# Second layers of experts 1 to 7 on column tiles of 64 and 32 tokens, in an attention and mixture-of-experts kernel

## The chip, the cores and the metric

The kernel runs on one core of a Trainium2 chip. The metric is the device time of one execution in microseconds (us); the time before is the median of three runs.

## The reference

Attention with normalised queries and keys feeds a mixture of experts that keeps, for each of 8 experts, the 80 tokens with the largest gate weight. All other rows of the output are zero.

```python
# q, k, v: (8, 12, 448, 64) f32;  x = attention output as (N=3584, D=768)
q_n, k_n = rmsnorm(q, g_q), rmsnorm(k, g_k)
attn = softmax(q_n @ k_n.T / sqrt(64));  x = attn @ v

logits = x @ w_gate                        # (3584, 8)
expert_idx = argmax(logits, axis=1);  gate_w = softmax(logits)[chosen expert]
for e in range(8):
    tok_idx = tokens of expert e, at most the 80 with the largest gate_w
    h = maximum(x[tok_idx] @ w1[e], 0)     # (80, 768) @ (768, 1024)
    out[tok_idx] = gate_w[tok_idx] * (h @ w2[e])   # (80, 1024) @ (1024, 768)
```

## The kernel before

The program has three stages. The first, about 350 us long, is the attention: it goes over 24 groups of four heads, with TensorE in tiles of 64 rows by 64 columns for the scores (`ps`) and the weighted values (`po`), and in tiles of 64 by 32 for the gate's logits (`zl`). Meanwhile GpSimd's queue brings the weights of experts 0 to 2 into SBUF as bf16 and stages those of experts 3 to 7 in DRAM as bf16 (`wb_scratch`, function `stage_w`). The second stage, some 12 us, ranks the tokens of the last batch, forms for each expert the list of its 80 tokens (`idxG`, `idxT`) and their gate weights (`gwT`), and picks expert 0's tokens with matmuls (`chosen`, tile `xT`). Matmuls called `busy` (tile `hot`) compute nothing that is used; they keep TensorE at work in the gaps.

The third stage is the loop over the experts, and the change lies there. For each expert e:

- `gather` fetches the 80 token rows (780 f32 each) from DRAM by an indirect DMA of GpSimd's queue, up to four experts ahead.
- `normal` scales the rows into bf16 (`xn`, three VectorE operations), and `xpose` turns them with six TensorE transposes (`pxt`) and a copy into `xgT`.
- First layer: 48 matmuls, w1's 128x128 blocks as weights and the 80 tokens as the moving side, into `ph`; ScalarE's Relu makes `h_sb` in two halves.
- Second layer: 16 matmuls, `h_sb`'s eight blocks (128 rows x 80 tokens) as weights and 384 columns of w2 as the moving side, into two `py` tiles of 80 x 384. Expert 7's runs as 32 matmuls of 192 columns.
- `weighted` multiplies by the gate weight on VectorE (`yo`), and `scatter` writes the 80 rows to the output by an indirect DMA.

All orders are those of the code; the schedule is manual, and each engine runs its instructions in that order. The weights of experts 6 and 7 go into the buffers of experts 0 and 1, in transfers of SyncE's queue that each wait until the old weights have been read (`fetch_late`). Their staged copies are written and read in the order (chunk, partition, column), so that one piece of DRAM is one row of a block: 2048 bytes for w1, 1536 for w2.

Of the kernel before, what the change touches and what calls it, by code (L numbers as in the profile page):

```python
# [21 lines left out]
def kernel(  # L22
# [41 lines left out]
    NW0 = 3  # L64
# [99 lines left out]
    def constants():  # L164
# [2 lines left out]
        nc.vector.tensor_scalar(numI[:, 1, :], rowI[:, :NJ + 1], 15, None, op0=ALU.bitwise_and)  # L167
        nc.vector.tensor_copy(numF[:, :, :], numI[:, :, :])

    onesb = tpool.tile([CAP, 128], BF16, name="onesb")  # L170
    nc.gpsimd.memset(onesb[:, :], 1.0)

# [26 lines left out]
    def load_weights(pool, e, slot, early=None):  # L199

        w1 = []
        for n, (c0, c1) in enumerate(((0, DC), ) if early is None else ((0, NE), (NE, DC))):
            if n == 0 and early is not None:
                w1.append(early)
                continue
            w1.append(pool.tile([128, c1 - c0, F], BF16, tag=f"w1_{slot}", name="w1_sb"))
        w2_sb = pool.tile([128, FC, DM], BF16, tag=f"w2_{slot}", name="w2_sb")
        w_tiles[e] = (w1, [w2_sb])

    def chunk(e, i, c):  # L210
        ts = w_tiles[e][i]
        return ts[0][:, c] if len(ts) == 1 or c < NE else ts[1][:, c - NE]
# [55 lines left out]
    with av_stack:  # L268
# [521 lines left out]
        def at_slot(where, s, f, *a):  # L790
            where.setdefault(s, []).append((f, a))
# [85 lines left out]
        for g in (NG - 2, NG - 1):  # L877
            at_slot(end, NS, xstore, g)
        at_slot(mid, 1, constants)
        for i in range(N // 128):  # L880
# [209 lines left out]
    for cs in (((3, 4, 1), (4, 5, 1)), ((0, 3, 0), )):  # L1090
# [7 lines left out]
        if cs[0][0]:  # L1098
# [8 lines left out]
    outs = dram_disjoint_views(out, E + 1)  # L1107
    xgs = {}
    def gather(e, wait=False):

        if e == 1:
            xgs[e] = tpool.tile([128, 1024], F32, tag="beat", name="xg")[:CAP, :XW]
        elif e % 4 == 3:
            xgs[e] = prep.tile([128, NJ + 1, 256], F32, tag="xb", name="xg")[
                :CAP].rearrange("p j d -> p (j d)")[:, :XW]
        else:
            xgs[e] = upool.tile([128, 2, S], F32, tag="us", name="xg")[:CAP].rearrange(
                "p u s -> p (u s)")[:, :XW]
        if wait:
            nc.vector.memset(xgs[e][:, 0:1], 0.0)  # L1120
        nc.gpsimd.indirect_dma_start(
            out=xgs[e], out_offset=None, in_=xr_dram[:, :],
            in_offset=bass.IndirectOffsetOnAxis(ap=idxG[:, e:e + 1], axis=0))

    gather(1)
    idxT = tpool.tile([CAP, E], U32, name="idxT")
    nc.vector.tensor_copy(idxT[:, :], psc[:CAP, 1, :E])
    idxL = tpool.tile([CAP, 2], U32, tag="move", name="idxL")
    for half in range(2):
        nc.vector.tensor_scalar(idxL[:, half:half + 1], psc[:CAP, 1, E - 1:E], 2.0, float(half),  # L1130
                                op0=ALU.mult, op1=ALU.add)
    gwT = tpool.tile([CAP, E], F32, name="gwT")
    nc.vector.reduce_sum(out=gwT[:, :], in_=psc[:CAP, 0, :3 * E].rearrange("p (c e) -> p e c", c=3),
                         axis=AX.X)
    busy(1)
    chosen(2, False)
    busy(1)
    for i in range(3):
        chosen(i, True)
    busy(2)  # L1140
    xgT = mpool.tile([128, DC, CAP], BF16, tag="xgT", name="xgT")

    def by_two(x, ps):
# [3 lines left out]

    by_two(xgT, [t[:, 0, :DC // 2 * CAP] for t in xT])
    xts = {0: xgT}
    ps_stack.close()  # L1150
    mps = ctx.enter_context(tc.tile_pool(name="moe_ps", bufs=2, space=PSUM, reuse_waits="tile"))


    def normal(e, behind=None):
        xg = xgs[e]
        xn = mpool.tile([CAP, DM], BF16, tag="xn", name="xn")
        for i in range(NQ):
            nc.vector.tensor_mul(*rows_normal(i, xn, xg))
            if behind and not i:
                behind()  # L1160
        return xn
# [15 lines left out]
            by_two(xgT, [first, pxt[:, :DC // 2].rearrange("p c t -> p (c t)")])  # L1177
        xts[e] = xgT

    def sums(pw):  # L1180
        return [mps.tile([CAP, pw], F32, tag=("py", "py", "pz", "pxt")[i], name="py",
                         bufs=2 if i < 2 else 1) for i in range(DM // pw)]

    pys = sums(DM // 2)
    for e in range(2, 4):
        gather(e, wait=(e == 2))
    for e in range(E):
        h_sb = mpool.tile([128, FC, CAP], BF16, tag="hsb", name="h_sb")
        for fh in range(2):
# [10 lines left out]
        if e + 1 < E and e != 1:  # L1200
            xn = normal(e + 1, (lambda: fetch_part(slice(FE, FC), True)) if not e else None)
        if 0 < e < E - 1:
            xpose(e + 1, xn)
        if e < E - 4:
            gather(e + 4, wait=True)
        DN = DM // 2
        yo = mpool.tile([CAP, DM], F32, tag="yo", name="yo", bufs=3)

        def scatter(half=None):
            if half is None:  # L1210
                o, at, y, n = outs[e], idxT[:, e:e + 1], yo[:, :], N
            else:
                o = outs[e + half].rearrange("n (h d) -> (n h) d", h=2)
                at, y, n = idxL[:, half:half + 1], yo[:, half * DN:half * DN + DN], 2 * N
            nc.gpsimd.indirect_dma_start(  # L1215
                out=o[:, :], out_offset=bass.IndirectOffsetOnAxis(ap=at, axis=0),
                in_=y, in_offset=None, bounds_check=n - 1, oob_is_err=False)

        pw = DN if e + 1 < E else DN // 2
        if e:  # L1220
            pys = sums(pw)

        def product(i, fcs):
            for fc in fcs:
                nc.tensor.matmul(pys[i][:, :], h_sb[:, fc, :],  # L1225
                                 chunk(e, 1, fc)[:, i * pw:i * pw + pw],
                                 start=(fc == 0), stop=(fc == FC - 1))

        def weighted(i):
            nc.vector.tensor_scalar(yo[:, i * pw:i * pw + pw], pys[i][:, :], gwT[:, e:e + 1],  # L1230
                                    None, op0=ALU.mult)

        if e + 1 < E:
            for fh in range(2):
                for i in range(2):
                    if not e and fh and i:
                        xpose(1, xn)
                    product(i, range(fh * (FC // 2), (fh + 1) * (FC // 2)))
            if not e:
                xn = normal(2)  # L1240
            for i in range(2):
                weighted(i)
            scatter()
        else:
            for fh in range(2):
                for i in range(2):
                    product(i, range(fh * (FC // 2), (fh + 1) * (FC // 2)))
                    if fh:
                        weighted(i)
            scatter(0)  # L1250
            for i in range(2, 4):
                product(i, range(FC))
                weighted(i)
            scatter(1)
        if NW0 + 3 + e < E:
            load_weights(wpool, NW0 + 3 + e, e)
            fetch_late(NW0 + 3 + e)


# [33 lines left out]
```

## Time and profile before

| | |
|---|---|
| median of three runs | 408.78 us (408.08 to 409.58) |
| the profiled execution's own time | 408.54 us |
| its span, first to last instruction | 406.8 us |
| busy, share of the span: TensorE matmuls | 97% |
| VectorE / ScalarE / GpSimd | 86% / 79% / 21% |
| granted TensorE clock, mean over the span | 0.996 |
| DMA over the span | 248 GB/s mean |

Busy shares are averages over stages with different limits. The loop over the experts takes the span's last 42 us, from 365 us on. The trace names each instruction by engine, line, operation and tiles; a matmul's recorded length holds its way through the array, so that starts are what tells the pace.

### The profile page before, as it was taken

The page shows a single profiled execution, that of the slowest core. Times are in us where ns is not written, and L with a number is a line of the kernel's source. Part 1 is how long each engine was busy: PE and PEld are TensorE (multiplying, and loading weights), DVE is VectorE, ACT ScalarE, POOL GpSimd, SP SyncE. Part 2 cuts the span into 40 slices and gives each one's busy share as a digit, 9 for nine tenths or more (in the row PEclk, how much of TensorE's full clock was granted, in tenths as well). Part 3 has the DMA queues.
Part 4 walks back from the last instruction along what each step waited for, and adds up shares of the span by engine and source line. Part 5 has one row for each costly group of instructions (what it writes and reads, how often), then busy time and mean ns, then how long its engine had stood idle before and what let it go on. Part 6 is the DMA issues. An engine that isn't in the chain of part 4 may idle for free.

```text
span 406.8 us, 12614 instructions
## 1 busy us (share of the span) xinstructions
PE 395.8 (97%) x5284; PEld 196.0 (48%) x5284; DVE 351.7 (86%) x655; ACT 321.2 (79%) x510; POOL 86.8 (21%) x142
## 2 busy tenths in 40 slices
PE   8999999999999999999999999999999999999994
PEld 7434444444444444444444443444444444468884
DVE  4899987998999999997999999979999977876552
ACT  5898979997989879987899789979897878482110
POOL 6200002401032012320251024010520020144422
PEclk9999999999999999999999999999999999999998
DMA  7358999999989999979999999999999459898991
GB/s 245 127 174 197 280 288 262 282 205 310 243 236 257 258 262 255 295 172 258 243 305 220 245 269 231 289 238 278 232 287 256 134 166 377 262 280 264 342 348 53
DMA packets 76041, 100.92 MB, mean 248 GB/s; under 512 B 8385, under 2 KB 65217, under 8 KB 75985
## 3 DMA queue, kind: packets, MB, share of 16 engines
q1 hardware_dynamic: 60176, 70.99, 54.2%
q0 software_dynamic: 15808, 29.13, 39.4%
q8 instruction: 41, 0.67, 0.6%
q14 instruction: 16, 0.12, 0.1%
HBM read 101.11 MB, written 39.89 MB: 347 GB/s over the span
## 4 chain that ended last, share of the span: by engine, by line
PE 73%; DVE 12%; ACT 8%; issue 5%; POOL 2%; POOLq 0%; DVEq 0%
PE ps L425 26%; PE po L442 25%; PE zl L477 5%; DVE sm L460 4%; PE tp L383 4%; PE xp L383 3%; DVE ms L316 2%; DVE qn L346 2%; PE py L1225 2%; PE wps L896 2%; POOL out_dram L1215 2%; ACT at L428 1%; PE ph L1194 1%; ACT qkT L414 1%; PE mp L668 1%
## 5 line engine op out<-in xcount | busy, mean ns | idle before, releaser
L428 ACT ACTIVATE at<-ps 128x896 f32<-128x896 f32 x168 | 146.5, 930 | 4.5 <-PE ps L425 3.3
L425 PE MATMUL ps<-qkT 64*64 64x448 f32 x1344 | 147.3, 548 | 2.5 <-ACT row L626 1.3
L442 PE MATMUL po<-at,vt 64*64 64x448 f32 x1344 | 142.5, 537 | 0.0
L460 DVE TENSOR_TENSOR sm<-sm,at 128x896 f32<-128x896 f32 x120 | 130.7, 1089 | 3.1
L442 PEld LDWEIGHTS po<-at,vt 64*64 64x64 f32 x1344 | 50.1, 133 | 74.0 <-issue 63.9
L425 PEld LDWEIGHTS ps<-qkT 64*64 64x64 f32 x1344 | 43.8, 132 | 66.6 <-issue 26.3
L316 DVE TENSOR_REDUCE ms<-sq 128x14 f32<-128x896 f32 (+1 forms) x50 | 52.0, 1042 | 6.8 <-ACT sq L309 6.7
L346 DVE TENSOR_TENSOR qn<-qk,rs 128x896 f32<-128x896 f32 (+1 forms) x47 | 50.6, 1078 | 1.3
L309 ACT ACTIVATE sq<-qk 128x896 f32<-128x896 f32 (+1 forms) x48 | 44.7, 930 | 2.1 <-DMA qk<-in_q_dram 1.1
L229 POOL COPY mark<-mark 1x1 bf16<-1x1 bf16 x18 | 7.1, 394 | 131.8 <-DVE mark L228 131.8
L745 ACT COPY xb<-xp 128x1024 f32<-128x1024 f32 x24 | 24.3, 1012 | 8.4 <-PE xp L383 8.1
L383 PEld LDWEIGHTS tp<-ident,qn 64*128 64x128 f32 x672 | 23.5, 139 | 12.1 <-issue 5.3
L383 PE MATMUL tp<-ident,qn 64*128 64x64 f32 x672 | 27.2, 226 | 0.3 <-DVE qn L346 0.3
L1198 ACT ACTIVATE h_sb<-ph 128x320 bf16<-128x320 f32 x16 | 7.0, 437 | 25.4 <-PE ph L1194 25.4
L449 ACT COPY us<-po 128x896 f32<-128x896 f32 (+1 forms) x24 | 21.4, 894 | 6.5 <-PE po L442 6.4
L458 DVE TENSOR_TENSOR sm<-at 128x896 f32<-128x896 f32 x24 | 26.0, 1083 | 0.1
L414 ACT COPY qkT<-tp 128x896 f32<-128x896 f32 x24 | 22.0, 917 | 3.6 <-PE tp L383 3.5
L412 ACT ACTIVATE qkT<-tp,gqk 128x896 f32<-128x896 f32 x23 | 23.6, 1025 | 0.0
L1225 PE MATMUL py<-w_sb,h_sb 128*80 128x384 bf16 (+1 forms) x144 | 22.4, 309 | 0.0
L1230 DVE TENSOR_SCALAR yo<-py,gwT 80x384 f32<-80x384 f32 (+1 forms) x18 | 10.0, 568 | 12.0 <-PE py L1225 11.9
L477 PE MATMUL zl<-us,wgs 64*32 64x448 f32 x192 | 20.3, 540 | 0.0
L477 PE MATMUL zl<-sm,zsel 64*32 64x448 f32 x192 | 20.1, 540 | 0.0
(202 smaller groups left out, 431.1 us busy)
## 6 DMA issues: line engine op xcount, KB each, us to landing
w_sb<-wb_scratch SPq DMA_DIRECT2D x8, 1536.0 KB, 11.5
vt<-in_v_dram SPq DMA_DIRECT2D x24, 448.0 KB, 7.1
out_dram<-zeros SPq DMA_DIRECT2D x28, 384.0 KB, 9.0
qk<-in_q_dram SPq DMA_DIRECT2D x23, 448.0 KB, 6.9
qk<-in_k_dram SPq DMA_DIRECT2D x23, 448.0 KB, 6.2
w_sb<-in_moe_w_dram POOLq DMA_DIRECT2D x6, 1536.0 KB, 15.2
xr_scratch<-xb SPq DMA_DIRECT2D x48, 192.0 KB, 6.8
wb_scratch<-in_moe_w_dram POOLq DMA_DIRECT2D x12, 768.0 KB, 9.7
```

The costliest lines, as they stand in the source:

```text
L309: nc.scalar.activation(o, x, AF.Square)
L316: nc.vector.reduce_sum(out=st[g]["ms"][:, a, lo:hi], in_=st[g]["sq%d" % a][:, lo:hi], axis=AX.X)
L346: e.tensor_mul(qn[:].rearrange("p (x hh) d -> p hh x d", hh=2)[:, h0:h1], qk[:, lo:hi].rearrange("p (hh x) d -> p hh x d", x=NX), rs[:, lo ...
L383: nc.tensor.transpose(o, w, one[p, p], tile_position=(p.start, 0))
L414: nc.scalar.copy(T[:], tp[:, :, :S])
L425: nc.tensor.matmul(ps[u * 64:u * 64 + 64, hh, :S], T1[d, u, x * 64:(x + 1) * 64], T0[d, u, :], start=True, stop=True)
L428: nc.scalar.activation(at[:], ps[:, :, :S], AF.Exp)
L442: nc.tensor.matmul(po[u][hh * D:(hh + 1) * D, u, :S], vt[p, hh * NX + x, :], at[p, hh, :], start=(x == 0), stop=(x == RD - 1))
L458: nc.vector.tensor_add(s["sm"][:], s["at0"][:], s["at1"][:])
L460: nc.vector.tensor_add(s["sm"][:], s["sm"][:], s["at%d" % x][:])
L477: nc.tensor.matmul(t[32 * c:32 * c + 32, r, :S], w, x, start=(i == 0), stop=(i == NQ - 1))
L1225: nc.tensor.matmul(pys[i][:, :], h_sb[:, fc, :], chunk(e, 1, fc)[:, i * pw:i * pw + pw], start=(fc == 0), stop=(fc == FC - 1))
```

## The change

**Second layers.** Experts 1 to 7 no longer use weights of 128 rows x 80 tokens. The first 64 tokens run as `main`: weights of 64 columns in two column tiles of the array, the left one for w2's columns 0 to 383, the right one for 384 to 767; both write one `py` tile of 128 partitions. The last 16 tokens run as `rest`, once for two experts (1 and 2, 3 and 4, 5 and 6): weights of 32 columns (tokens 48 to 79) in four column tiles, two for each expert, each with 384 columns of w2, into one `pz` tile. Expert 7's rest has four tiles of 192 columns. Tokens 48 to 63 are computed twice and are not written the second time: their row numbers are pushed out of bounds (`SKIP`).

**Lists.** Gate weights and row numbers are needed in the new partition order. Six f32 matmuls with slices of the identity spread them (`spread`), ahead of expert 0's first layer; one `busy` matmul there goes.

**Order.** The gathers of experts 2 and 3 come after the first half of expert 0's first layer (a VectorE copy that reads `ph`). `normal(e + 2)` stands in expert e, ahead of the product's scaling. Expert 7's w2 is fetched after expert 2's rest, in two parts.

**DRAM layout.** The staged weights of experts 6 and 7 lie as (partition, chunk, column): one run of 12288 bytes for each partition.

```diff
+    MT = 64
+    LT = CAP - 32
+    SKIP = float(1 << 17)
     def staged(e, i):
-        return wb_dram[e - NW0, i].rearrange("(c p f) -> p c f", p=128, c=(DC, FC)[i])
+        return wb_dram[e - NW0, i].rearrange(
+            "(p c f) -> p c f" if e >= E - 2 else "(c p f) -> p c f", p=128, c=(DC, FC)[i])
...
+    psp = [hot[-1][:, 1, :2 * E], hot[-1][:, 1, 2 * E:3 * E]]
+    for o, c in enumerate((slice(0, MT), slice(LT, CAP))):
+        n = c.stop - c.start
+        for p in range(0, 128, n):
+            es = slice(1 + p // 64, None, 2) if o else slice(0, E)
+            nc.tensor.matmul(psp[o][p:p + n].rearrange("p (c e) -> p c e", c=2), ident[:CAP, c],
+                             rows[:, :, es], start=(o == 0), stop=(o == 1))
...
+    def main(e, py, fcs):
+        for fc in fcs:
+            for n in range(2):
+                product(py[MT * n:MT * n + MT, :], e, fc, slice(0, MT),
+                        slice(n * DN, n * DN + DN))
+
+    def rest(parts, pz, fcs):
+        w = len(parts) * DM // 4
+        for fc in fcs:
+            for n in range(4):
+                e, c = parts[n * len(parts) // 4], n % (4 // len(parts)) * w
+                product(pz[32 * n:32 * n + 32, :w], e, fc, slice(LT, CAP), slice(c, c + w))
...
+            if e == fh == 0:
+                gather(2, ph[:CAP, 0, 0:1])
+                gather(3)
...
+        if 0 < e < E - 2:
+            xn = normal(e + 2)
...
         else:
+            py = sums("py")
+            main(e, py, fcs)
+            yo = mpool.tile([128, DN], F32, tag="yo", name="yo", bufs=3)
+            nc.vector.tensor_scalar(yo[:, :], py[:, :], gws[:, e:e + 1], None, op0=ALU.mult)
+            scatter(e, idxM[:, e:e + 1], yo[:, :], 2)
+        if e and (e % 2 == 0 or e == E - 1):
+            k = (e - 1) // 2
+            pair = (e - 1, e) if e < E - 1 else (e, )
+            w = len(pair) * DM // 4
+            pz = sums("pz")
+            rest(pair, pz, fcs)
...
+        elif e == 2:
+            w2 = wpool.tile([128, FC, DM], BF16, tag="w2_1", name="w2_sb")
+            w_tiles[E - 1][1].append(w2)
+            for c in (slice(0, FE), slice(FE, FC)):
+                nc.sync.dma_start(out=w2[:, c], in_=staged(E - 1, 1)[:, c])
```

On TensorE, at the end of expert 2's second layer, the program before has these rows (py_6102 and py_6103 are its two halves of 80 x 384; LDWEIGHTS loads the weights of the matmul below it; ph_6126 is expert 3's first layer):

```order
L1225 LDWEIGHTS h_sb_6032
L1225 MATMUL py_6102<-w2_sb_125,h_sb_6032 80x384
L1225 LDWEIGHTS h_sb_6032
L1225 MATMUL py_6103<-w2_sb_125,h_sb_6032 80x384
...
L1194 LDWEIGHTS w1_sb_5200
L1194 MATMUL ph_6126<-xgT_6089,w1_sb_5200 128x80
```

The changed program has there (py_6129 is expert 2's main tile, py_6151 the rest tile of experts 1 and 2; w2_sb_124 and h_sb_5967 are expert 1's, w2_sb_126 and h_sb_6060 expert 2's):

```order
L1225 LDWEIGHTS h_sb_6060
L1225 MATMUL py_6129<-w2_sb_126,h_sb_6060 64x384
L1225 LDWEIGHTS h_sb_5967
L1225 MATMUL py_6151<-w2_sb_124,h_sb_5967 32x384
L1225 LDWEIGHTS h_sb_5967
L1225 MATMUL py_6151<-w2_sb_124,h_sb_5967 32x384
L1225 LDWEIGHTS h_sb_6060
L1225 MATMUL py_6151<-w2_sb_126,h_sb_6060 32x384
```

Sixteen rows of 80x384 for each expert have become sixteen of 64x384 for each and thirty-two of 32x384 for the two, and the w2 of the expert before is still read here.

On VectorE, from the end of the second stage into expert 1, the program before has these rows (L1158 is `normal`, L1146 and L1175 are `xpose`'s copies, L1120 the write that a gather waits for, L1230 the scaling):

```order
L1133 TENSOR_REDUCE gwT<-psc 80x8
L1146 CAST xgT<-xT 128x240
L1120 MEMSET xg 80x1
L1158 TENSOR_TENSOR xn<-xg 80x2x2x64
L929 MEMSET w_sb 128x1
L1158 TENSOR_TENSOR xn<-xg 80x2x2x64 x2
L1120 MEMSET xg 80x1
L1146 COPY xgT<-pxt 128x240
L1158 TENSOR_TENSOR xn<-xg 80x2x2x64 x3
L1230 TENSOR_SCALAR yo<-py,gwT 80x384 x2
L1175 COPY xgT<-pxt 128x480
```

And the changed program, from the same place on (L1135 is the copy that holds back the gather of expert 2, L1189 `normal`, L1279 the scaling of expert 0, L1286 that of a main):

```order
L1168 CAST xgT<-xT 128x240
L1172 COPY spread<-hot 128x24
L1175 TENSOR_SCALAR idxM<-spread,off 128x8
L1179 TENSOR_SCALAR idxP<-spread,off 128x3
L1179 TENSOR_SCALAR idxP<-spread,off 128x1
L1135 COPY xg<-ph 80x1
...
L1279 TENSOR_SCALAR yo<-py,rows 80x384 x2
L1206 COPY xgT<-pxt 128x480
L1133 MEMSET xg 80x1
L1189 TENSOR_TENSOR xn<-xg 80x2x2x64 x3
L1286 TENSOR_SCALAR yo<-py,spread 128x384
```

The write that released expert 2's gather has become a copy that must wait for `ph`, and in expert 1 the rows of expert 3 are normalised ahead of expert 1's scaling.

On GpSimd's queue each scatter of a main or a rest has 128 row numbers, of which those of the tokens computed twice are out of bounds; there are 12 scatters (one of expert 0, seven of mains, four of rests) in place of 9.

## Rows read from the trace of the kernel before

**Rows 1.** Window of expert 3: each engine's busy time and instructions.

```profile
378.80:383.40 4.60, 4.60 (x77) 3.85 (x74) 2.68 (x9) 0.88 (x2) 2.13 (x2) 1.00 1.04 307
```

Columns: the window and its length, then PE, PEld (weight loads), DVE, ACT, POOL, each with its instructions, the granted clock (1.00 is full), the DMA engines' busy share, and GB/s.

**Rows 2.** The chain that ended last: start and length in us, what.

```profile
344.69 1.50 PE po L442 x16
...
369.67 1.72 PE ph L1194 x48
371.39 0.22 PE pxt L1173 x6
371.61 2.60 PE py L1225 x16
```

**Rows 3.** Timeline around 344 us, TensorE alone: start, length, engine, line, operation.

```profile
342.96 1.73 PE L425 MATMUL ps<-qkT 64*64 64x448 f32 x16
344.51 1.68 PE L442 MATMUL po<-at,vt 64*64 64x448 f32 x16
346.13 0.18 PE L668 MATMUL mp<-eqb,tied 128*128 128x8 bf16 x1
...
346.77 0.56 PE L477 MATMUL zl<-us,wgs 64*32 64x448 f32 x1
...
347.93 0.54 PE L477 MATMUL zl<-sm,zsel 64*32 64x448 f32 x1
...
348.43 1.74 PE L442 MATMUL po<-at,vt 64*64 64x448 f32 x16
```

The tile's form stands ahead of the operand's: 64*32 is 64 rows by 32 columns of the array.

**Rows 4.** Timeline, all engines: weight loads of the zl matmuls and of 80 columns.

```profile
346.80 0.11 PEld L477 LDWEIGHTS zl<-sm,zsel 64*32 64x32 f32 x2
...
353.61 0.40 PEld L710 LDWEIGHTS <-keep 80*80 80x80 bf16 x8
```

**Rows 5.** Timeline ahead of expert 0's first layer.

```profile
364.41 0.60 PE L603 MATMUL hot<-tri,identb 128*128 128x512 bf16 x2
...
364.61 0.41 DVE L1146 CAST xgT<-xT 128x240 bf16<-128x240 f32 x1 [0.28 <-PE xT L1082]
...
364.91 1.93 PE L1194 MATMUL ph<-xgT,w_sb 128*128 128x80 bf16 x48
```

**Rows 6.** Timeline of gathers 2 and 5, expert 2's `normal`, and expert 3's scaling.

```profile
365.31 0.90 POOL L1121 DMA_INDIRECT xg<-xr_scratch,idxG  x1 [1.11 <-DVE xg L1120]
...
369.25 1.08 DVE L1158 TENSOR_TENSOR xn<-xg 80x256 bf16<-80x256 f32 x3
...
372.93 0.93 POOL L1121 DMA_INDIRECT xg<-xr_scratch,idxG  x1 [0.30 <-issue]
...
382.72 1.26 DVE L1230 TENSOR_SCALAR yo<-py,gwT 80x384 f32<-80x384 f32 x2 [1.54 <-PE py L1225]
```

**Rows 7.** DMA issues, last number us to landing: gathers 2, 4, 5; expert 7's w2.

```profile
xg<-xr_scratch,idxG POOLq DMA_INDIRECT x1, 3.5
...
xg<-xr_scratch,idxG POOLq DMA_INDIRECT x1, 8.6
...
xg<-xr_scratch,idxG POOLq DMA_INDIRECT x1, 7.6
...
w_sb<-wb_scratch SPq DMA_DIRECT2D x1, 1536.0 KB, 22.9
```

**Rows 8.** Timeline of SyncE's last transfer and of the tail.

```profile
374.24 1.95 SPq L244 DMA_DIRECT2D w_sb<-wb_scratch  x1
...
398.62 2.87 PE L1225 MATMUL py<-w_sb,h_sb 128*80 128x192 bf16 x32
...
399.88 0.74 DVE L1230 TENSOR_SCALAR yo<-py,gwT 80x192 f32<-80x192 f32 x2 [2.16 <-PE py L1225]
...
400.90 0.92 POOL L1215 DMA_INDIRECT out_dram<-yo,idxL  x1 [1.99 <-DVE yo L1230]
401.53 0.41 DVE L1230 TENSOR_SCALAR yo<-py,gwT 80x192 f32<-80x192 f32 x1 [0.25 <-PE py L1225]
402.84 0.92 POOL L1215 DMA_INDIRECT out_dram<-yo,idxL  x1 [1.02 <-DVE yo L1230]
```

More of the change, by code (lines that the diff above doesn't have):

```diff
@@ L879 @@
         at_slot(mid, 1, constants)
+        at_slot(mid, 3, offsets)
         for i in range(N // 128):
@@ L1106, with gather @@
             chosen(1, False)
-    outs = dram_disjoint_views(out, E + 1)
+    outs = dram_disjoint_views(out, E + E // 2)
     xgs = {}
-    def gather(e, wait=False):
+    def gather(e, behind=None, wait=False):
         if e == 1:
@@ L1120, in gather @@
             nc.vector.memset(xgs[e][:, 0:1], 0.0)
+        if behind is not None:
+            nc.vector.tensor_copy(xgs[e][:, 0:1], behind)
         nc.gpsimd.indirect_dma_start(
@@ L1125 @@
     gather(1)
[L1126 to L1134, printed above, removed]
+    idxT = tpool.tile([CAP, 1], U32, name="idxT")
+    nc.vector.tensor_copy(idxT[:, :], psc[:CAP, 1, :1])
+    rows = tpool.tile([CAP, 2, E + 1], F32, tag="move", name="rows")
+    nc.vector.tensor_copy(rows[:, 1, :E], psc[:CAP, 1, :E])
+    nc.vector.reduce_sum(out=rows[:, 0, :E],
+                         in_=psc[:CAP, 0, :3 * E].rearrange("p (c e) -> p e c", c=3), axis=AX.X)
+    nc.vector.tensor_copy(rows[:, :, E:], rows[:, :, E - 1:E])
+    gwT = rows[:, 0]
     busy(1)
@@ L1178, in xpose, with sums, scatter, product @@
         xts[e] = xgT
[L1180 to L1186, printed above, removed]
+    DN = DM // 2
+    def sums(tag, p=128, n=DN):
+        return mps.tile([p, n], F32, tag=tag, name="py", bufs=2 if tag == "py" else 1)
+    def scatter(k, at, y, h):
+        o = outs[k] if h == 1 else outs[k].rearrange("n (h d) -> (n h) d", h=h)
+        nc.gpsimd.indirect_dma_start(
+            out=o[:, :], out_offset=bass.IndirectOffsetOnAxis(ap=at, axis=0),
+            in_=y, in_offset=None, bounds_check=h * N - 1, oob_is_err=False)
+    hs = {}
+    def product(o, e, fc, t, c):
+        nc.tensor.matmul(o, hs[e][:, fc, t], chunk(e, 1, fc)[:, c],
+                         start=(fc == 0), stop=(fc == FC - 1))
+    def main(e, py, fcs):
[6 more added lines that the diff above has]
+        for fc in fcs:
+            for n in range(4):
+                e, c = parts[n * len(parts) // 4], n % (4 // len(parts)) * w
+                product(pz[32 * n:32 * n + 32, :w], e, fc, slice(LT, CAP), slice(c, c + w))
+    pys = [sums("py", CAP) for _ in range(2)]
     for e in range(E):
         h_sb = mpool.tile([128, FC, CAP], BF16, tag="hsb", name="h_sb")
+        hs[e] = h_sb
         for fh in range(2):
@@ L1205 @@
             gather(e + 4, wait=True)
[L1206 to L1231, printed above, removed]
@@ L1233 @@
-        if e + 1 < E:
+        if 0 < e < E - 2:
+            xn = normal(e + 2)
+        fcs = range(FC)
+        if e == 0:
+            yo = mpool.tile([CAP, DM], F32, tag="xo", name="yo", bufs=1)
             for fh in range(2):
                 for i in range(2):
-                    if not e and fh and i:
+                    if fh and i:
                         xpose(1, xn)
-                    product(i, range(fh * (FC // 2), (fh + 1) * (FC // 2)))
-            if not e:
-                xn = normal(2)
+                    for fc in fcs[fh * (FC // 2):(fh + 1) * (FC // 2)]:
+                        product(pys[i][:, :], e, fc, slice(0, CAP), slice(i * DN, i * DN + DN))
+            xn = normal(2)
@@ L1241 @@
             for i in range(2):
-                weighted(i)
-            scatter()
-        else:
[L1245 to L1257, printed above, removed]
+                nc.vector.tensor_scalar(yo[:, i * DN:i * DN + DN], pys[i][:, :], gwT[:, :1],
+                                        None, op0=ALU.mult)
@@ new lines @@
+            scatter(0, idxT[:, :1], yo[:, :], 1)
+        else:
+            py = sums("py")
[9 more added lines that the diff above has]
+            rest(pair, pz, fcs)
+            last = e == E - 1
+            yr = mpool.tile([128, DN], F32, tag="yo" if last else "yr", name="yr",
+                            bufs=3 if last else 1)
+            nc.vector.tensor_scalar(yr[:, :w], pz[:, :w], gwP[:, k:k + 1], None, op0=ALU.mult)
+            scatter(E + k, idxP[:, k:k + 1], yr[:, :w], 4 // len(pair))
```

28 lines of the change are left out of this document (25 added, 3 removed).

## The prediction

> **What bounds the kernel now.** I read the windows first, because the change touches the loop over the experts and little else. In the window of expert 3 TensorE is busy 4.60 of 4.60 us at a granted clock of 1.00, while VectorE has 2.68, ScalarE 0.88 and GpSimd 2.13 us of work [rows 1]. So TensorE sets the pace of an expert. The chain that ended last says how its 4.5 us divide: 1.72 for the first layer, 0.22 for the transposes, 2.60 for the second layer [rows 2]. Sixteen matmuls in 2.60 us are 162.5 ns each, the time to stream 384 columns; every one of them costs that, with 80 columns of weights or with 32.
>
> The DMA engines come second: in the same window their share is 1.04 [rows 1], that is, full. Their last work that matters is expert 7's w2, issued at 374.24 and landed 22.9 us later, at 397.1, and its reader starts at 398.62 [rows 7, 8]. TensorE can thus gain 1.5 us ahead of expert 7 before this transfer could hold it, even if the new layout gives nothing. In the tail neither bounds: the last scatter starts at 402.84, 0.90 us after its data is ready (401.53 and 0.41), and the one ahead of it at 400.90 [rows 8].
>
> **The change part by part.**
>
> *Streams.* What the main and the rest cost depends on whether column tiles that share all rows of the array run at once. No bf16 matmul of 128 rows does this here, but the gate's logits come near: tiles of 64x32, four of them side by side on the same rows, eight at once. Three rounds of eight take 347.93 - 346.77 = 1.16 us, 0.387 each [rows 3]; the sixteen `po` of 64x64 tiles, four at once, add 1.50 to the chain [rows 2], 0.375 for a round of four. So four column tiles of a row group do run together, at some 3% more than a stream. Two or four tiles of bf16 should then take the 162.5 ns of one matmul, and up to 10 ns more: I take 170. The weight loads fit: eight loads of 80 columns lie within 0.40 us, a recorded length of about 0.1 us included, some 43 ns apart [rows 4], and four of 32 columns have 162 ns. A main is 8 rounds, 1.36 us; a rest is 8 rounds, 1.36 us, for two experts. Two experts now cost 5.20 us of second layers, and then 2 x 1.36 + 1.36 = 4.08: 1.12 less. Three pairs give **-3.36** (at 162.5 ns -3.90, at 180 ns -2.64).
>
> *Changes of form.* The program now goes from whole to 64-column to 32-column tiles and back. A pair has five such changes (two for the odd expert, three for the even one), three pairs have 15. The attention has such seams: from `po` to a whole-array matmul 346.13 - 344.51 - 1.50 = 0.12 us, from `zl` to `po` 348.43 - 347.93 - 0.375 = 0.125 [rows 3]. But `ps` to `po`, with no change of form, also takes 1.55 us for 1.50 of streams, 0.05 [rows 3]. So a change costs between 0.07 and 0.125; I take 0.11, near the two seams that do change. 15 x 0.11 = **+1.65** (1.05 to 1.9).
>
> *Ahead of expert 0.* Six small f32 matmuls in two forms replace one `busy`. The second `busy` streams until about 364.84 (two of 0.21 from 364.41), and the first layer starts at 364.91 and waits for VectorE's copy until 365.02 [rows 5]. Three changes of form at 0.11 and six matmuls at 0.04 (the spacing of the small loads in [rows 4]) are 0.57; without the 0.21 of the `busy`, TensorE comes 0.36 later, of which 0.07 to 0.18 were idle. **+0.2** (0 to 0.5). The lists' own VectorE operations come behind that copy, and ahead of `normal(1)`, which waits for its gather; they are hidden.
>
> *The later gather 2.* It was issued at 365.31, and took 3.5 us, landing at 368.8; `normal(2)` ran at 369.25 [rows 6, 7]. Now it waits for half a first layer of a later expert 0, and starts at about 366.7. With 3.5 us it lands at 370.2, 0.9 us past 369.25 (less about 0.2 by which all is later). `normal(2)` is then late; behind it on VectorE stand expert 0's two scalings, and the first main needs the PSUM buffer that the first of these frees. Before, that buffer was free about 0.6 us ahead of its use (369.25 + 1.08 + half of an operation pair of 1.26 is 370.96, against a second layer that starts at 369.67 + 1.72 + 0.22 = 371.6). So the stall is 0 to 0.3 at that length, nothing if the gather, alone on the queue now, lands sooner, and up to 0.85 if it takes 4.2 or so. **+0.1** (0 to 0.85).
>
> *Order of `normal`.* It stands an expert earlier on VectorE, ahead of a scaling. Gather 5, issued at 372.93 with 7.6 us [rows 6, 7], lands at 380.5; its new place comes at about 380, and its transposes at about 383.2. A late gather now holds back a scaling too, but the next main has a second PSUM buffer. Nothing.
>
> *Expert 7 and the tail.* From the start of its second layer to the last scatter it was 402.84 - 398.62 = 4.22 us. Now: a change 0.11, main 1.36, about 0.2 through the array, a scaling of 0.6 (half of the 1.26 of [rows 6]), 0.28 to the scatter, as from 400.62 (399.88 and 0.74) to 400.90 before [rows 8]: main's scatter at 2.55. The rest's last data is ready at about 3.2 (eight rounds of four loads, 0.10 to 0.13 each). Its scatter then waits for GpSimd: the two scatters before stood 1.94 apart, and two gathers can stand 1.2 apart. That is 3.75 to 4.49, against 4.22. A scatter of 128 row numbers in place of 80 may take 0.92 to 1.47 us. Together -0.5 to +0.8; **0**, between the ends.
>
> *DRAM layout, constants.* Longer runs may bring the weights sooner; nothing waits for them (above), so 0. If w2 came at the old time and TensorE gained more than 1.5 us, the cover would end, but its first part (six of eight blocks) lands earlier, and the last two are read 1 us into the main. The constants are 16 small GpSimd writes in the attention, where GpSimd is busy 21% of the span.
>
> Sum: -3.36 + 1.65 + 0.2 + 0.1 + 0 = **-1.4**. The profiled execution took 408.54, so 407.1; the median of the runs stands 0.24 higher, so **407.4**.
>
> **The rivals.**
>
> *The seams eat it.* With 180 ns a round, 0.125 a change, 0.5 ahead of expert 0, 0.5 at gather 2 and +0.5 in the tail: -2.64 + 1.9 + 1.5 = +0.8, 409.5; with half of these, about 408.4. For it: each is within its bounds. Against: all must lean one way.
>
> *Cheaper seams.* 0.07 a change, 162.5 ns, and 1.2 us between the last scatters: -3.9 + 1.05 + 0.1 - 0.5 = -3.2, 405.5. Against it: both seams with a change of form show 0.12.
>
> *Starved gathers (the other side).* A gather lands 3.5 us after its issue on quiet DMA engines, and 7.6 to 8.6 beside the weights [rows 7]. The weights' pieces of 1.5 to 2 KB become runs of 12 KB. If a gather's pieces must then wait longer between them, gathers 4 to 7 land late. Gather 5's transposes leave it about 9 us (383.2 - 1.1 - 372.9); each microsecond of landing beyond is one of stall for `xpose`, where TensorE waits with nothing behind it that it may do. At 10.4 us the gain is gone, at 11.6 the kernel is 0.3% slower, and at 13 it is 411.2. Against: the bytes are the same, and the queue of weights then ends sooner. The Trainium skill, "DMA: Bandwidth & Descriptors", section on queues, rings and completion order, has each DMA engine take turns between queues packet by packet, which speaks for this rival; the trace has no long packets beside gathers, so no run here shows it.
>
> *Tiles one after another.* If a weight load waited for the matmul on the same rows, each small matmul would cost its stream and its load: main 16 x 0.19, rest 32 x 0.19, 12.2 us for a pair in place of 5.2: +21 for three pairs, and expert 7's +4, near 434. Against: the loads of `zl`'s next round stand at 346.80, while the first round, on the same rows, runs until 347.17 and beyond [rows 3, 4]. By the Trainium skill, "TensorE: Matmul & The Clock Gate", Part 3, loads overlap matmuls in flight only when the row group differs, which would be this rival; the trace does not agree.
>
> **How the numbers follow.** Forecast 0.50 (406.4 to 408.2), seams 0.22, cheaper seams 0.13, starved 0.12, one after another 0.03. About 0.3%, 1.2 us, is what a measurement here can tell from no change. The forecast's 0.50 splits 0.37 to 0.13 at 407.55; cheaper seams are all faster; the seams are 0.18 same and 0.04 slower; starved 0.02 same and 0.10 slower. Faster 0.50, same 0.33, slower 0.17. For 8 in 10 the range leaves out the far ends of starved gathers and the last rival, 0.1, and a tail of the cheap end, 0.1: **405.6 to 409.9**.
>
> **What would show it.** Right: mains of about 1.36 us and rests of about 1.36, with starts of the two or four tiles together; seams of 0.1; TensorE without gaps from expert 1 on; expert 7's second layer about 1.4 us earlier. Wrong: a wait of transposes for `xn` and behind it for a gather; a start of expert 7's main that waits for w2; last scatters 2 us apart or more; starts of column tiles one stream apart.

## The result and the profile after

The changed kernel took 412.58 us (median of four runs, 412.18 to 412.83), the kernel before beside it 408.66 (408.08 to 409.58): a ratio of 1.0084, 95% interval 1.0057 to 1.0111. It is slower by 0.8%; the forecast had it 0.3% faster. The profiled execution took 412.54 us, 4.0 more than that of before, with a span of 410.8 and a granted clock of 0.998.

The timeline of the changed kernel, rows of the loop over the experts (start, length, engine, line; in brackets the idle time before it and what ended it). L1250 is the first layer, L1225 main and rest, L1204 the transposes, L1189 `normal`, L1206 the copy into `xgT`, L1297 the scaling of a rest, L1136 a gather, L1218 a scatter:

```profile
365.21 1.90 PE L1250 MATMUL ph<-xgT,w_sb 128*128 128x80 bf16 x48
366.70 0.91 POOL L1136 DMA_INDIRECT xg<-xr_scratch,idxG  x1 [2.44 <-DVE xg L1135]
...
372.11 1.49 PE L1225 MATMUL py<-w_sb,h_sb 128*64 128x384 bf16 x16 [0.20 <-DVE yo L1279]
...
373.54 1.90 PE L1250 MATMUL ph<-xgT,w_sb 128*128 128x80 bf16 x48
374.13 0.93 POOL L1136 DMA_INDIRECT xg<-xr_scratch,idxG  x1 [0.30 <-issue]
...
376.37 2.90 PE L1225 MATMUL py<-w_sb,h_sb 128*64 128x384 bf16 x48
...
377.79 1.09 PEld L1225 LDWEIGHTS <-h_sb 128*32 128x32 bf16 x32 [0.30 <-issue]
...
379.21 0.46 PE L1250 MATMUL ph<-xgT,w_sb 128*128 128x80 bf16 x8
...
383.76 0.93 POOL L1136 DMA_INDIRECT xg<-xr_scratch,idxG  x1 [0.30 <-issue]
...
385.73 1.09 DVE L1189 TENSOR_TENSOR xn<-xg 80x256 bf16<-80x256 f32 x3 [3.97 <-DMA xg<-xr_scratch,idxG]
...
386.21 0.92 PE L1204 MATMUL pxt<-identb,xn 80*128 80x80 bf16 x6 [1.65 <-DVE xn L1189]
...
394.64 0.62 DVE L1297 TENSOR_SCALAR yr<-py,spread 128x384 f32<-128x384 f32 x1 [2.00 <-DMA out_dram<-yr,idxP]
395.17 0.40 DVE L1206 COPY xgT<-pxt 128x480 bf16<-128x480 bf16 x1
395.62 1.88 PE L1250 MATMUL ph<-xgT,w_sb 128*128 128x80 bf16 x48 [1.78 <-DVE xgT L1206]
...
397.16 1.09 DVE L1189 TENSOR_TENSOR xn<-xg 80x256 bf16<-80x256 f32 x3 [1.59 <-DMA xg<-xr_scratch,idxG]
...
403.15 2.27 PE L1225 MATMUL py<-w_sb,h_sb 128*64 128x384 bf16 x48
...
405.58 0.98 POOL L1218 DMA_INDIRECT out_dram<-yo,idxM  x1 [2.26 <-DVE yo L1286]
406.86 0.98 POOL L1218 DMA_INDIRECT out_dram<-yr,idxP  x1 [0.30 <-issue]
```

TensorE's work came out as the sum had it. A main runs from 372.11 to 373.54, 1.43 us with the change of form behind it; a main and a rest from 376.37 to 379.21, 2.84. The time went to waits that were not there before. Expert 5's rows are normalised only at 385.73, when their gather of 374.13 has landed, and TensorE stands 1.65 us ahead of the transposes. At 394.64 a rest's scaling waits 2.00 us for the scatter that still reads its buffer; the copy into `xgT` is queued behind it on VectorE, and the first layer of expert 6 stands 1.78 us. Where `xn` comes late the six transposes also follow `normal`'s three operations two by two and take 0.8 to 0.9 us (386.21) in place of 0.4; this happens four times, for experts 3, 5, 6 and 7, and is some 2 us more. From the first layer of expert 0 to expert 7's second layer it is 37.94 us (365.21 to 403.15), against 33.71 before [rows 5, 8]; the tail, to the last scatter, is 3.71 against 4.22. The loop's stretch is thus 4.23 longer, and with the tail and a start 0.30 later, 4.23 - 0.51 + 0.30 = 4.0, which is the whole difference.

What the gathers cost, in the view of the tile `xg` of the changed kernel (idle time of VectorE, and all recorded landings):

```profile
  DMA xg<-xr_scratch,idxG: 15.5, 7
...
DMA to landing us min/median/max: 3.6/9.9/12.6
```

Before, VectorE waited 2.2 us, once, for a gather. The DMA issues of the changed kernel, last number us to landing: gathers 2, 5 and 6, the scatter of the first rest (issued 382.45), the last part of expert 7's w2 (issued near 379.8):

```profile
xg<-xr_scratch,idxG POOLq DMA_INDIRECT x1, 3.6
...
xg<-xr_scratch,idxG POOLq DMA_INDIRECT x1, 11.5
...
xg<-xr_scratch,idxG POOLq DMA_INDIRECT x1, 12.6
...
out_dram<-yr,idxP POOLq DMA_INDIRECT x1, 12.1
...
w_sb<-wb_scratch SPq DMA_DIRECT2D x1, 384.0 KB, 19.0
```

Gather 5 took 7.6 before [rows 7], and now 11.5. The last part of w2 landed near 398.8, against 397.1 before; but this w2 was also issued five us later, at 379.3 and after, behind expert 2's rest, where it had been 374.24 [rows 8]. Whether longer pieces by themselves come sooner is read from e2 below.

### The profile page after: what moved, and what is told of

Same layout as the page of the kernel before. It is cut to its first block, busy times and chain, and to the rows that moved or that the text cites. A ratio compares the mean times of both kernels' runs of the same rounds, so it can differ in the third digit from the quotient of the medians.

```text
span 410.8 us, 12889 instructions
## 1 busy us (share of the span) xinstructions
PE 394.6 (96%) x5407; PEld 191.6 (47%) x5407; DVE 350.3 (85%) x654; ACT 320.9 (78%) x510; POOL 90.2 (22%) x161
## 4 chain that ended last, share of the span: by engine, by line
PE 65%; DVE 11%; issue 8%; ACT 7%; POOL 4%; DMA 3%; POOLq 0%; DVEq 0%
PE ps L437 26%; PE po L454 25%; PE zl L489 5%; PE tp L395 3%; DVE sm L472 3%; PE xp L395 3%; POOL out_dram L1218 2%; DVE ms L328 2%; DVE qn L358 2%; DMA xr_scratch<-xb 2%; ACT at L440 1%; ACT xb L757 1%; DMA xr_scratch<-rz 1%; POOL xg L1136 1%; DMA xg<-xr_scratch,idxG 1%
## 5 line engine op out<-in xcount | busy, mean ns | idle before, releaser
L1189 DVE TENSOR_TENSOR xn<-xg 80x256 bf16<-80x256 f32 x21 | 7.7, 417 | 15.5 <-DMA xg<-xr_scratch,idxG 15.5
L395 PEld LDWEIGHTS xp<-ident,us 64*128 64x128 f32 x384 | 14.0, 139 | 12.0 <-ACT at L440 10.6
## 6 DMA issues: line engine op xcount, KB each, us to landing
w_sb<-wb_scratch SPq DMA_DIRECT2D x7, 1536.0 KB, 11.5
```

Of the source, the lines that this page charges most:

```text
L395: nc.tensor.transpose(o, w, one[p, p], tile_position=(p.start, 0))
```

## The experiments

Sixteen kernels ran, in four sets; each set has its own runs of the kernel before on the same chip, and the ratios are to those. The second and the third set ran on one chip.

| kernel | pieces, bytes | ratio | 95% interval |
|---|---|---|---|
| first set, before 408.62 us | | | |
| e1: change with the old layout | 2048, 1536 | 1.0005 | 0.9988 to 1.0022 |
| e2: before with the new layout | 12288 | 1.0050 | 1.0034 to 1.0067 |
| e3: change, a buffer more for a rest | 12288 | 1.0096 | 1.0068 to 1.0124 |
| e4: change, two chunks a transfer | 4096, 3072 | 0.9979 | 0.9958 to 1.0000 |
| second set, before 409.74 us | | | |
| f1: e4 with early gathers | 4096, 3072 | 1.0012 | 0.9989 to 1.0035 |
| f2: change with early gathers | 12288 | 1.0083 | 1.0056 to 1.0109 |
| f3: e1 with early gathers | 2048, 1536 | 1.0020 | 0.9994 to 1.0045 |
| d3: change, half-length pieces | 6144 | 1.0020 | 0.9994 to 1.0046 |
| third set, before 409.76 us | | | |
| g1: e4 again | 4096, 3072 | 1.0006 | 0.9980 to 1.0032 |
| g2: before, two chunks a transfer | 4096, 3072 | 1.0008 | 0.9993 to 1.0023 |
| g3: f1 again | 4096, 3072 | 1.0014 | 0.9992 to 1.0037 |
| g4: d3 again | 6144 | 1.0014 | 0.9990 to 1.0038 |
| fourth set, before 410.02 us | | | |
| h1: change, no late weights | none | 1.0030 | 1.0011 to 1.0049 |
| h2: before, no late weights | none | 1.0010 | 0.9992 to 1.0028 |
| h3: before | 2048, 1536 | 0.9995 | 0.9983 to 1.0007 |
| h4: e4 a third time | 4096, 3072 | 0.9989 | 0.9971 to 1.0007 |

### The layout, away and alone

**e1** takes the layout out of the change; **e2** puts it alone into the kernel before (the same two lines the other way).

```diff
     def staged(e, i):
-        return wb_dram[e - NW0, i].rearrange(
-            "(p c f) -> p c f" if e >= E - 2 else "(c p f) -> p c f", p=128, c=(DC, FC)[i])
+        return wb_dram[e - NW0, i].rearrange("(c p f) -> p c f", p=128, c=(DC, FC)[i])
```

> The changed kernel, but the staged weights of experts 6 and 7 lie and travel as before, in pieces of 2048 and 1536 bytes. Theory A (the 12288-byte pieces hold back the gathers and scatters on the DMA engines): the gathers land again after 7.6 to 8.6 us in place of 9.9 to 12.6, TensorE's waits for expert 5's and expert 7's rows and for the rest's buffer go, and the time is 406.8 to 408.0. Rival B (the later gather of expert 2, the earlier normal and the three more scatters are late whatever the layout): 411.5 to 413.

> The kernel before with only the new DRAM layout of experts 6 and 7. Theory A: gathers land after 10 to 12.6 us where they took 7.6 to 8.6; expert 5's rows were needed about 10.8 us after their gather was issued, so TensorE waits 0 to 2 us there and the time is 408.8 to 411. Rival B: the layout is innocent, 408.2 to 408.9, or faster if expert 7's w2 lands sooner.

Without the layout the 0.8% are gone; alone, with no column tile in the program, it costs 0.5%. The tile `xg` in the kernel before with the new layout alone:

```profile
  DMA xg<-xr_scratch,idxG: 3.7, 3
...
DMA to landing us min/median/max: 3.4/10.1/13.2
```

The landings have gone from 3.5/7.6/8.6 in the kernel before to this, by the layout alone, and the transposes of experts 6 and 7 now come behind a late `xn`; at the second of them TensorE waits:

```profile
395.28 0.92 PE L1174 MATMUL pxt<-identb,xn 80*128 80x80 bf16 x6 [0.36 <-DVE xn L1159]
```

The weights themselves landed sooner. The second and the third of the late transfers, issued at the same times to within 0.1 us, took before:

```profile
w_sb<-wb_scratch SPq DMA_DIRECT2D x1, 1536.0 KB, 16.7
...
w_sb<-wb_scratch SPq DMA_DIRECT2D x1, 1536.0 KB, 21.0
```

and in e2:

```profile
w_sb<-wb_scratch SPq DMA_DIRECT2D x1, 1536.0 KB, 14.2
...
w_sb<-wb_scratch SPq DMA_DIRECT2D x1, 1536.0 KB, 18.5
```

The trace's records of single pieces say how long one holds its engine: 0.47 us in the median for one of 12288 bytes in e2, 0.07 and 0.08 for those of 1536 and 2048 before. A gather's rows are 48 such records, three for each of 16 engines if evenly spread. If each waited for one long piece in place of a short one, that would be about 1.2 us (an estimate); the median landing moved by 2.5 and the longest by 4.6, so this alone is not enough, and no run shows what the rest is.

In e1 the landings are 3.8/7.5/10.0. e1 did not reach the forecast, though. In its profiled execution (411.66 us, where its median is 408.8) gather 3, issued at 367.14, landed ten us later, and TensorE waited:

```profile
377.08 1.09 DVE L1188 TENSOR_TENSOR xn<-xg 80x256 bf16<-80x256 f32 x3 [4.75 <-DMA xg<-xr_scratch,idxG]
...
377.56 0.98 PE L1203 MATMUL pxt<-identb,xn 80*128 80x80 bf16 x6 [2.71 <-DVE xn L1188]
...
378.47 5.38 PE L1224 MATMUL py<-w_sb,h_sb 128*64 128x384 bf16 x48
```

The main and rest behind the wait take 5.38 us, against 2.90 in the changed kernel: the windows of e1 show why (granted clock, DMA share and GB/s are last):

```profile
374.00:379.00 5.00, 2.25 (x34) 1.47 (x32) 1.92 (x7) 0.88 (x2) 0.50 (x2) 0.78 1.03 270
379.00:383.00 4.00, 4.00 (x38) 1.81 (x38) 1.72 (x6) 0.00 (x0) 2.75 (x3) 0.50 1.06 338
```

### The rest's buffer

**e3** gives the rest of experts 3 and 4 a buffer of its own, so that its scaling need not wait for the scatter before it.

```diff
-            yr = mpool.tile([128, DN], F32, tag="yo" if last else "yr", name="yr",
-                            bufs=3 if last else 1)
+            yr = mpool.tile([128, DN], F32, tag="yo" if last else ("yr", "xo", "yr")[k],
+                            name="yr", bufs=3 if last else 1)
```

> The changed kernel with a buffer of its own for the rest of experts 3 and 4, so that its scaling does not wait until the scatter of the rest of experts 1 and 2 has landed. Theory A: the wait of 1.8 us ahead of expert 6's first layer goes, but the rows of expert 7, which landed at 397.1 in the changed kernel, hold TensorE at nearly the same point: 411.5 to 412.6. Rival C (that buffer is the cause of its 1.8 us): 410.8.

412.0 us, against 412.58 for the change itself, and ratios whose intervals overlap: no gain can be told. In its trace the wait for the scatter is gone, and expert 7's transposes wait 0.64 us for their rows, as had been expected. But this execution also waits 2.03 us for expert 3's rows, which the change's trace does not, with a granted clock of 0.67 in the window 377.4 to 381.5 behind it. So what the buffer is worth was not measured.

### Shorter pieces in the new layout

**e4** keeps the layout and splits each late transfer.

```diff
-                nc.sync.dma_start(out=ts[0][:], in_=staged(e, i))
+                n = 2 if e >= E - 2 else ts[0].shape[1]
+                for h in range(0, ts[0].shape[1], n):
+                    nc.sync.dma_start(out=ts[0][:, h:h + n], in_=staged(e, i)[:, h:h + n])
...
-            for c in (slice(0, FE), slice(FE, FC)):
-                nc.sync.dma_start(out=w2[:, c], in_=staged(E - 1, 1)[:, c])
+            for c in range(0, FC, 2):
+                nc.sync.dma_start(out=w2[:, c:c + 2], in_=staged(E - 1, 1)[:, c:c + 2])
```

> The changed kernel with the new DRAM layout, but the weights of experts 6 and 7 fetched by transfers of two chunks each, in pieces of 4096 bytes for w1 and 3072 for w2. Theory A with the length of a piece as the cause: gathers land between the two, 8 to 10 us, and the time lies at 407.5 to 410. If the place in DRAM is the cause and not the length of a piece, or if rival B holds: 411.5 to 413.

The same bytes at the same place, and the landings are those of before. Tile `xg` of e4:

```profile
DMA to landing us min/median/max: 3.4/7.7/8.5
```

TensorE in e4:

```profile
364.47 1.89 PE L1252 MATMUL ph<-xgT,w_sb 128*128 128x80 bf16 x48
...
369.07 1.88 PE L1252 MATMUL ph<-xgT,w_sb 128*128 128x80 bf16 x48
...
374.66 2.90 PE L1227 MATMUL py<-w_sb,h_sb 128*64 128x384 bf16 x48
377.50 1.90 PE L1252 MATMUL ph<-xgT,w_sb 128*128 128x80 bf16 x48
...
396.58 0.84 PE L1227 MATMUL py<-w_sb,h_sb 128*64 128x384 bf16 x8
397.73 0.52 PE L1227 MATMUL py<-w_sb,h_sb 128*64 128x384 bf16 x4 [0.30 <-DMA w_sb<-wb_scratch]
398.70 1.29 PE L1227 MATMUL py<-w_sb,h_sb 128*64 128x384 bf16 x36 [0.46 <-DMA w_sb<-wb_scratch]
```

From 364.47 to 396.58 it is 32.11 us, 1.60 less than before: what the sum had for the loop (three pairs at -0.57, gather 2's +0.1), reached in this execution. What comes next is the cover that the prediction named: expert 7's second layer waits for its w2, 0.30 and 0.46 us. This w2 is issued from 379.68 on, against 374.24 before. The profiled execution took 406.85, the median is 407.89.

### Later gathers, and pieces of half the length

**f1**, **f2** and **f3** put the gathers of experts 2 and 3 back ahead of expert 0's first layer, in e4, in the change and in e1; **d3** uses pieces of 6144 bytes (`n = (3, 4)[i]`, w2 by four chunks).

```diff
+    for e in range(2, 4):
+        gather(e, wait=(e == 2))
...
-            if e == fh == 0:
-                gather(2, ph[:CAP, 0, 0:1])
-                gather(3)
```

> The kernel with two-chunk pieces, and the gathers of experts 2 and 3 put back to where they were, ahead of expert 0's first layer. Theory A2 (after the long pieces are gone, the later gather 3 still costs TensorE a wait in some executions, and a clock at half speed behind it): 406.5 to 407.6, with fewer high runs than the 405.9 to 410.4 of the two-chunk kernel. Rival D (the place of these two gathers is indifferent; expert 7's w2, which held TensorE for 0.8 us, is the rest): 407.5 to 408.3.

> The changed kernel with its 12288-byte pieces, and only the gathers of experts 2 and 3 put back ahead of expert 0's first layer. Theory A (long pieces hold back the gathers of experts 4 to 7): 411 to 412.6, nearly as the changed kernel. Rival B2 (the later place of gathers 2 and 3 pushes all later gathers back, and that is the loss): 407.5 to 409.

> The changed kernel with the old DRAM layout (pieces of 2048 and 1536 bytes) and the gathers of experts 2 and 3 put back ahead of expert 0's first layer: column tiles and order of normal remain. Theory A2: the 2.7 us wait for expert 3's rows and the half clock behind it, seen with the old layout alone, go: 406.5 to 407.8. Rival D: 408.4 to 409.2, as with the old layout alone.

> The changed kernel with the new DRAM layout, fetched in halves: pieces of 6144 bytes. Theory A with the length as the cause: the later gathers land after 8.5 to 11 us, between 7.8 at two-chunk pieces and 11.5 at whole ones, and the time lies between the two, 408 to 411. If a transfer's issue or the number of transfers mattered and not the length, it would be 407.9 or below.

f2 has the loss of the change itself (1.0083, 1.0084), so the later gathers do not cause it; f1, which differs from f2 only in the split transfers and ran on the same chip, does not have it (1.0012). f1 and f3 missed both of their forecasts: they stood 0.33% and 0.15% worse than e4 and e1 in the first set. The next set was to tell the chip from the edits.

**g1**, **g3** and **g4** are e4, f1 and d3 again on one chip, which was that of the second set; **g2** is e2 with the split transfers of e4.

> The changed kernel with the new DRAM layout, fetched two chunks at a time (pieces of 4096 and 3072 bytes), once more, now on the same chip as the other three. Theory A (long pieces hold back the gathers; without them the column tiles bring the 1.6 us that the profile showed, less a wait for expert 7's w2): 0.996 to 1.000 of the kernel before. Rival E (the 0.998 was that chip; on the second chip every version was 0.2 to 0.3% worse against the kernel before): within 0.15% of the version with early gathers beside it.

> The kernel before (weights of 80 tokens, its own order), with only the new DRAM layout, fetched two chunks at a time. Theory A: with short pieces nothing waits, and nothing is gained, since TensorE sets the pace: 0.999 to 1.002 against the kernel before, where 12288-byte pieces gave 1.005. Rival F (the 0.998 of the changed kernel with these pieces came from the pieces, not from the column tiles): 0.997 to 0.999.

> The version with two-chunk pieces and the gathers of experts 2 and 3 back ahead of expert 0's first layer, on the same chip as the version with the later gathers. If their earlier place costs time: 0.2 to 0.4% above that version, and in the profile the Relu of expert 0's first half starts some 2 us after its matmuls, as it did on the second chip. Rival E (that was the chip): equal to within 0.15%, both with such stalls or both without.

> The changed kernel with pieces of 6144 bytes, on the same chip as the pieces of 4096 and 3072. Theory A (the longer the pieces, the later the gathers): 0.2 to 0.5% above the two-chunk pieces, the later gathers landing 8.5 to 11 us after issue. Rival (only pieces of 12288 bytes hurt): equal to within 0.15%, landing near 8.

g1, g3 and g4 lie within 0.08% of each other: the second set's difference was not the gathers' place, and pieces of 6144 bytes cannot be told from shorter ones by the time (the traces of d3 and g4 record no landing of a gather). Only 12288 bytes stand apart. g2 shows the layout harmless in the kernel before once the pieces are short (1.0008, where e2 had 1.0050), and that it brings nothing. `staged` gives the order of the writes to DRAM as well as of the reads, and g2 keeps both; so the writes are not the cause either.

### No late weights

**h1** and **h2** leave out the transfers of the weights of experts 6 and 7, and compute these two experts with the weights of experts 0 and 1. h3 is the kernel before, h4 is e4.

```diff
+        if e < 2:
+            w_tiles[E - 2 + e] = w_tiles[e]
```

> The changed kernel without the transfers of the weights of experts 6 and 7: these two experts are computed with the weights of experts 0 and 1, which lie in SBUF. So no weights move in the loop, whatever the length of their pieces. Theory A (the sum is right for TensorE, and what it gains is lost to the transfers beside it): 1.4 us, 0.34%, below the kernel before without these transfers, beside it here, with gathers that land within 5 us and no wait of TensorE. Rival G (column tiles cost TensorE something that the sum lacks): within 0.15% of it or slower.

> The kernel before, likewise without the transfers of the weights of experts 6 and 7 (they are computed with those of experts 0 and 1). If the transfers cost the kernel before nothing, as the prediction had it: 0.999 to 1.001 against it. If they hold it up too: up to 0.3% faster.

> The kernel before, unchanged, to have its trace from the same chip as the others: 1.000. If the waits of ScalarE for TensorE that the changed kernel shows on the second chip, some 2 us past the matmuls, belong to that chip, this trace has them there too; if they come from the change, it has none wherever it runs.

> The changed kernel with pieces of 4096 and 3072 bytes a third time, beside the others. Theory A: between the kernel before and 1.4 us below it, 0.997 to 1.001. If this chip shows no late Relus, near the 0.998 of the first chip; if it does, near the 1.0006 of the second.

h2 agrees, within its interval, that the transfers cost the kernel before nothing. h1 contradicts the theory that they eat the rest of TensorE's gain: with none of them in the loop the column tiles are 0.2% slower than the kernel before without them. By their intervals this cannot be told from no change, but it is not the 0.34% faster of the theory. Its timeline, at expert 2:

```profile
373.34 1.72 PE L1250 MATMUL ph<-xgT,w_sb 128*128 128x80 bf16 x43
...
375.32 0.30 PE L1250 MATMUL ph<-xgT,w_sb 128*128 128x80 bf16 x4 [0.26 <-issue]
376.03 0.20 PE L1250 MATMUL ph<-xgT,w_sb 128*128 128x80 bf16 x1 [0.41 <-issue]
...
376.86 0.77 ACT L1257 ACTIVATE h_sb<-ph 128x320 bf16<-128x320 f32 x2 [4.61 <-PE ph L1250]
...
377.35 0.84 PE L1225 MATMUL py<-w_sb,h_sb 128*64 128x384 bf16 x8 [0.36 <-ACT h_sb L1257]
```

The Relu of the first half needs 24 matmuls, of which the last was started by 374.2 (43 start within 1.72 us); it runs at 376.86, together with that of the second half, and TensorE stands meanwhile for nothing that the profile names. The DMA share of the window 373 to 378 is 0.47 there. The kernel before has such a wait too on this chip (h3, expert 0's Relu):

```profile
364.95 1.93 PE L1194 MATMUL ph<-xgT,w_sb 128*128 128x80 bf16 x48
...
367.39 0.44 ACT L1198 ACTIVATE h_sb<-ph 128x320 bf16<-128x320 f32 x1 [2.49 <-PE ph L1194]
...
367.88 1.33 PE L1225 MATMUL py<-w_sb,h_sb 128*80 128x384 bf16 x7 [1.00 <-ACT h_sb L1198]
```

In the trace that the prediction read, it came 1.11 us after the first matmul of 364.91, and here 2.44:

```profile
366.02 0.44 ACT L1198 ACTIVATE h_sb<-ph 128x320 bf16<-128x320 f32 x1 [1.16 <-PE ph L1194]
```

In h3 TensorE has gaps of over 0.35 us between starts at two places in the loop, ahead of the second layer of expert 0 and within that of expert 7; in h1 at six, none of them behind a gather. In e4, on the first chip, there is one (0.49, ahead of 387.81), apart from those that wait for w2. The stretch from expert 0's first layer to expert 7's second is 33.71 us in the first trace of before and 34.90 in h3; with short pieces 32.11 in e4, 36.48 in g1 and 35.53 in h4; 36.75 in h1. So where these waits occur, the kernel before loses 1.2 us in this stretch and the changed one 3.4 to 4.4 (in h4 some 0.5 of it behind a late gather, expert 3's), and that is where the rest of the gain goes in these executions.

One part of the larger loss can be read from the rows. In h3 ScalarE stands 0.9 us between the Relus of the two halves in experts 2 to 6, where it stood 0.36 in the first trace. This costs nothing there: the eight matmuls that need only the first half last 1.3 us (eight of 162.5 ns, from 377.22 on in expert 2). Only in expert 7, whose first eight matmuls have 192 columns and last 0.8, does TensorE wait:

```profile
377.74 0.44 ACT L1198 ACTIVATE h_sb<-ph 128x320 bf16<-128x320 f32 x1 [0.92 <-PE pxt L1173]
...
400.60 0.44 ACT L1198 ACTIVATE h_sb<-ph 128x320 bf16<-128x320 f32 x1 [0.91 <-PE ph L1194]
...
401.09 2.17 PE L1225 MATMUL py<-w_sb,h_sb 128*80 128x192 bf16 x24 [0.41 <-ACT h_sb L1198]
```

A main's first eight matmuls are four rounds of two tiles, some 0.7 us, and so it waits in other experts too. In h4, expert 6 (its main starts at 395.19):

```profile
395.71 0.44 ACT L1259 ACTIVATE h_sb<-ph 128x320 bf16<-128x320 f32 x1 [0.99 <-PE pxt L1206]
...
396.20 2.25 PE L1227 MATMUL py<-w_sb,h_sb 128*64 128x384 bf16 x40 [0.17 <-ACT h_sb L1259]
```

Each such place costs some 0.3 us, and g1 and h1 have two of them, h4 this one; the larger waits, as that of expert 2 in h1, are not explained by it.

## Why the prediction was wrong, point by point

*The step that failed* is "DRAM layout, constants. Longer runs may bring the weights sooner; nothing waits for them (above), so 0". It asked who waits for the weights, and not who shares the DMA engines with them, though [rows 1] had these full. Pieces of 12288 bytes beside the gathers moved the median landing from 7.6 to 10.1 us with nothing else changed (e2), and cost the kernel before 0.50%; splitting the same transfers at the same place took this away (g2, 1.0008), and took the changed kernel from 1.0084 to 0.998 to 1.001 (e4, h4, g1).

*Its rival* "Starved gathers" is what happened; it had 0.12. Its mechanism and bound stood: gather 5 took 11.5 us, past the 9 that it had, and TensorE waited at the transposes. Its time for a landing of 13 was 411.2; the gathers of experts 5 to 7 took 11.5, 12.6 and, by the wait that it ended, 13.4, and it was 412.5, since a scatter's landing of 12.1 also held a rest's buffer, a wait that the rival did not have. (By its own bound, a landing of 13 is 4 us past 9 and gives 411.4 from 407.4.) What was put against it, "the bytes are the same, and the queue of weights then ends sooner", did not help: in e2 the weights did land sooner, by 2.5 us in two transfers, and the gathers beside them later all the same. The rule that spoke for it (the Trainium skill, "DMA: Bandwidth & Descriptors", section on queues, rings and completion order: turns between queues packet by packet) fits e2 and g2. How many pieces a queue sends in one turn no run shows.

*"Order of normal ... Nothing"* failed with it. With landings of 8 us it holds (in e4 no transpose waits for `xn`). At 11 us and more, `normal(e + 2)` is late and holds back on VectorE the main's scaling.

*Streams and changes of form* were right: a pair of experts from first layer to first layer takes 8.43 us in e4 (369.07 to 377.50), against 9.08 before (twice 4.54 [rows 2]). That is -0.65, where the sum had -1.12 + 0.55 = -0.57. The rival of tiles one after another is out. The Trainium skill, "TensorE: Matmul & The Clock Gate", Part 3, has loads overlap matmuls only when the row group differs; the 32 loads of a rest lie within 1.09 us, beside its matmuls on the same rows, so the trace does not agree.

*Ahead of expert 0 and the later gather 2*: the first layer started at 365.21, 0.30 later than before, where +0.2 stood. Gather 2 was issued at 366.70 and took 3.6, as worked out; the first main waited 0.20 for its buffer.

*Expert 7 and the tail*: 3.71 us against 4.22, the -0.5 end of the range, not 0: the last two scatters start 1.28 apart, and one of 128 row numbers takes 0.98 against 0.92.

*The cover of w2* ("TensorE can thus gain 1.5 us ahead of expert 7 before this transfer could hold it") was named and missized. It took the old issue at 374.24, while the change issues w2 only behind expert 2's rest, from 379.68 on in e4; at a gain of 1.6 us there w2 holds TensorE for 0.76, not for 0.1.

*What stays open.* By the ratios of the table the changed kernel with short pieces is 0.9979, 1.0006 and 0.9989 of the kernel before on three chips, not the 0.9966 of the sum; by their intervals no version here is surely faster than the kernel before. On the chips of the last three sets the late Relus take the difference in the traces. They are not the late weights' doing (h1). What delays them was not settled. Why the column tiles have more of them is settled only in part: a main reaches the second half of `h_sb` after 0.7 us in place of 1.3, a cover that the sum did not price. Transfers of instructions, a queue of their own in the profile, are no plain answer: in h3 none is under way during the wait of 366.5 to 367.4 (one ended at 365.9, the next began at 374.7). An intervention on these waits was not tried.

## What to carry to other kernels

A transfer for which nothing waits is not free: price what it does to the small transfers that share the engines, and look at their landings beside the slack of their readers, ahead of the bytes. When a layout makes the pieces of a bulk transfer longer, split the transfer first; two chunks at a time cost nothing here. Where a forecast is under half a per cent, run the kernel before on more than one chip: what an engine's trace gained on one (1.6 us) was not there on two others.

## What had not been expected of the hardware

- Pieces six to eight times as long brought the weights sooner and the gathers beside them later: in e2 two transfers of 1.5 MB landed after 14.2 and 18.5 us in place of 16.7 and 21.0, and the median gather after 10.1 in place of 7.6.
- After a wait of 2.71 us in e1 the granted clock was 0.50 for the window 379 to 383, the lower of the two levels (1.2 of 2.4 GHz), and a main and rest took 5.38 us in place of 2.90. Waits of 1.65 and 1.78 us in the changed kernel had no such sequel (1.00 in the windows 386 to 390 and 395.5 to 400).
- ScalarE's wait for TensorE can end some 2 us after the matmuls it needs were started, with a granted clock of 1.00 and without bulk transfers (h1), with the kernel before as with the changed one.
